# Retention in half chunks on 64x64 quarters of the TensorE array, beside a Strassen feed-forward network

## The chip, the cores and the metric

The kernel runs on 1 core of one Trainium2 chip. The metric is the device time in microseconds (us) of one execution, as a median over the runs of a kernel. A profile is one execution, so a profile's span and the median differ by a few us.

PE is TensorE, the engine for matrix products, and the *array* is what it multiplies in. DVE and ACT (VectorE and ScalarE) do sums, masks and copies, POOL is GpSimd. Transfers (DMA) bring data from memory (HBM) to the buffer beside the engines, whose 128 rows are called partitions; a *bank* is a part of the memory that PE writes its products to. In the profile each 32-bit product leaves two records and each transpose one; counts such as x32 are records.

## The reference, cut to what matters

Retention (attention with a decay in place of the softmax) for 8 batches, 8 heads, 576 positions, head size 64. Its output, as 4608 tokens of 512 features, goes through a feed-forward network with a squared ReLU:

```python
scores = scale * np.matmul(q, k.transpose(0, 1, 3, 2))      # (8, 8, 576, 576)
Dmat = np.where(rel >= 0, gamma[:, None, None] ** rel[None, :, :], 0.0)
x = np.matmul(scores * Dmat, v)                             # -> (4608, 512)
h = np.maximum(x @ w_in, 0.0)                               # w_in  (512, 2048)
out = h * h @ w_out                                         # w_out (2048, 512)
```

The kernel computes the network's matrix products by Strassen's scheme, seven products of blocks and some sums in place of eight products. All arrays that count here are 32-bit floats, except that the weights arrive as 64-bit floats and are converted on the chip.

## The kernel before

The retention runs by chunks of 128 positions, five a batch (the last has 64), 40 in all. For a chunk, x is the sum of two things: what lies within the chunk (masked scores times v) and what comes from all earlier chunks through a state u, which grows by k times v with each chunk. One *visit* of the outer loop does one piece of each of three neighbouring chunks, with pieces of the feed-forward network (`ffn`, made of steps h) and of the weight conversion (`convert`) between them:

```python
for i in range(N_CH + 2):
    if i >= 2:
        retain(i - 2)          # x of a chunk, then the growth of the state
        convert(2 if i < 6 else 1)
        ffn(i - 2)
    if 1 <= i <= N_CH:
        scores(i - 1)
        convert(1 if i > 1 else 0)
        ffn(i - 2)
    if i + 2 < N_CH:
        load(i + 2)            # q, k, v from HBM
    if i < 4:
        for j in range(...):   # (cut) the first weight pieces
            fetch_w(j)
    if i < N_CH:
        turn(i)                # transposes of q, then of k
        convert(1 if i > 1 else 0)
        ffn(i - 2)
```

The retention's products use half of the array: `scores` takes 64 rows by 128 columns (a head's 64 features are summed), x and the growth take 128 rows by 64 columns.

```python
def scores(i):
    # (cut)
    sc = [pool.tile([128, HP, C], F32, tag=tag, name=f"sc{e}") for e in range(2)]
    for hp in range(HP):
        for e in range(2):
            sl = slice(D * e, D * e + D)
            nc.tensor.matmul(sc[e][:cs, hp, :cs], lhsT=kT[sl, hp, :cs], rhs=qT[sl, hp, :cs], start=True, stop=True)
    # (cut) two masked copies by DVE into ret[0], ret[1]; GpSimd makes vs = v * decay

def retain(i):
    # (cut)
    for hp in range(HP):
        if ci > 0:
            for e in range(2):
                half = slice(D * e, D * e + D)
                nc.tensor.matmul(p[half, hp, :cs], lhsT=u_sb[ci % 2][:, hp, half], rhs=s["qT"][:, hp, :cs], ...)
        for e in range(2):
            half = slice(D * e, D * e + D)
            nc.tensor.matmul(p[half, hp, :cs], lhsT=s["vs"][:cs, 2 * hp + e, :], rhs=s["ret"][e][:cs, hp, :cs], ...)
    # (cut) ACT copies p to xT; then the 8 products of the growth, and ACT copies the state
```

The first weight matrix comes in 16 pieces of 512 KB, one transfer each:

```python
return moe_w_in.rearrange("(c p) f -> p c f", p=128)[:, :, f:f + 128]      # piece_src(j)
nc.sync.dma_start(raw_of(j).bitcast(I64)..., piece_src(j))                  # fetch_w(j)
```

Of the kernel before, what the change touches and what calls it, by code (L numbers as in the profile page):

```python
# [9 lines left out]
F32 = mybir.dt.float32  # L10
U32 = mybir.dt.uint32
I64 = mybir.dt.int64
AF = mybir.ActivationFunctionType
ALU = mybir.AluOpType

C = 128
TOK = 512
HT = TOK // 2

# [20 lines left out]
def kernel(  # L40
# [29 lines left out]



    nc = tc.nc
    ctx.enter_context(tc.manual_schedule())

    B, H, S, D = q.shape
    HP = H // 2
# [3 lines left out]
    N_DM = d_model // 128  # L81
# [6 lines left out]
    NCH = -(-S // C)  # L88
    chunks = [(b, ci, ci * C, min(C, S - ci * C)) for b in range(B) for ci in range(NCH)]
    N_CH = len(chunks)  # L90
# [8 lines left out]
    ld4 = first.enter_context(tc.tile_pool(name="ld4", bufs=4))  # L99
    work = first.enter_context(tc.tile_pool(name="work", bufs=1))  # L100
    work2 = first.enter_context(tc.tile_pool(name="work2", bufs=2))
    ps_a = first.enter_context(tc.tile_pool(name="ps_a", bufs=3, space=PS))
    ps_u = first.enter_context(tc.tile_pool(name="ps_u", bufs=1, space=PS))


# [18 lines left out]
    def load(i):  # L124
        b, ci, c0, cs = chunks[i]
        loaded[i] = []
        for name, src, pool in (("q", q, ld3), ("k", k, ld4), ("v", v, ld3)):
            t = pool.tile([128, H, D], F32, tag=name, name=f"{name}_ld")
            nc.sync.dma_start(t[:cs], src[b, :, c0:c0 + cs, :].rearrange("h s d -> s h d"))  # L129
            loaded[i].append(t)  # L130
            if i == 0 and name == "q":
                nc.sync.dma_start(dq[:, :, 0:C], decay_q[:, :, 0:C])
            if i == 0 and name == "k":
                nc.sync.dma_start(dv, decay_v)
        if i == 0:
            nc.sync.dma_start(dq[:, :, C:], decay_q[:, :, C:])
# [15 lines left out]
    def raw_of(j):  # L152
        return raw_all[j % N_RAW] if j < N_W1 else raw_all[(j - N_W1) % 3]
# [4 lines left out]
    def piece_src(j):  # L158
        wi, m, e = pieces[j]
        f = (m + e * N_M) * 128  # L160
        if wi == 0:
            return moe_w_in.rearrange("(c p) f -> p c f", p=128)[:, :, f:f + 128]
        return moe_w_out[f:f + 128, :].rearrange("p (c f) -> p c f", c=N_DM)

    def piece_dst(j):
# [6 lines left out]
    def as_dst(j, t):  # L172

        if pieces[j][0] == 0:
            return t.rearrange("p (c f) -> p c f", c=N_DM)
        return t.rearrange("p (o s f) -> p o s f", o=2, s=2)

    def fetch_w(j):
        if j < len(pieces) and wide:
            nc.sync.dma_start(raw_of(j).bitcast(I64).rearrange("p (c f) -> p c f", c=N_DM), piece_src(j))  # L180



# [1 line left out]
    def round_parts(j):  # L185
# [24 lines left out]
            nc.vector.scalar_tensor_tensor(bits, as_dst(j, hi), 0x80000000, bits, op0=ALU.bitwise_and, op1=ALU.bitwise_or)  # L210

        if not wide:
            return [lambda: nc.sync.dma_start(t, as_dst(j, piece_src(j).rearrange("p c f -> p (c f)")))] + [None] * 4
        return [one, two, three, four, five]

    def sum_w_in(mp):
# [65 lines left out]
    def convert(count):  # L282
        for _ in range(count):
            f = next(w_in_steps, None)
            f and f()
# [8 lines left out]
    ident = only.tile([128, 128], F32, name="ident")  # L294
    make_identity(nc, ident)

    msk = only.tile([128, 1, C], F32, name="msk")
    nc.gpsimd.memset(msk, 1.0)
    nc.gpsimd.affine_select(
        out=msk[:, 0, :], in_=msk[:, 0, :], compare_op=ALU.is_ge, fill=0.0, base=0,  # L300
        pattern=[[1, C]], channel_multiplier=-1,
    )

    u_sb = [only.tile([128, HP, 128], F32, name=f"u_sb{j}") for j in range(2)]
    for t in u_sb:
        nc.gpsimd.memset(t, 0.0)



# [3 lines left out]
    xT = {n: xT_room[n % 2 if n < 2 else (n - 3) % 2] for n in range(N_BLK)}  # L313
    xT[2] = W[6][:, 0:N_DM * TOK].rearrange("p (c t) -> p c t", c=N_DM)

    def turn(i):

        cs, c0 = chunks[i][3], chunks[i][2]
        for j, name in enumerate(("qT", "kT")):
            p = ps_a.tile([128, HP, C], F32, tag="a", name=f"{name}_ps")  # L320
            for hp in range(HP):
                nc.tensor.transpose(p[:, hp, :cs], loaded[i][j][:cs, 2 * hp:2 * hp + 2, :], ident[:cs, :cs])  # L322
            t = st[i][name] = (work if j else work2).tile([128, HP, C], F32, tag=name, name=name)
            if j == 0:
                nc.vector.tensor_tensor(t[:, :, :cs], p[:, :, :cs], dq[:, :, c0:c0 + cs], op=ALU.mult)
            else:
                nc.scalar.copy(t[:, :, :cs], p[:, :, :cs])

    def scores(i):

        b, ci, c0, cs = chunks[i]
        qT, kT = st[i]["qT"], st[i]["kT"]
        pool, tag = (ps_f, "f") if i < TOK // C else (ps_a, "a")
        sc = [pool.tile([128, HP, C], F32, tag=tag, name=f"sc{e}") for e in range(2)]
        for hp in range(HP):
            for e in range(2):
                sl = slice(D * e, D * e + D)
                nc.tensor.matmul(sc[e][:cs, hp, :cs], lhsT=kT[sl, hp, :cs], rhs=qT[sl, hp, :cs],  # L338
                                 start=True, stop=True)
        st[i]["ret"] = []  # L340
        for e in range(2):
            r = work.tile([128, HP, C], F32, tag=f"ret{e}", name=f"ret{e}")
            nc.vector.tensor_tensor(r[:cs, :, :cs], sc[e][:cs, :, :cs],  # L343
                                    msk[:cs, :, :cs].to_broadcast([cs, HP, cs]), op=ALU.mult)
            st[i]["ret"].append(r)
        vs = st[i]["vs"] = work.tile([128, H, D], F32, tag="vs", name="vs")
        nc.gpsimd.tensor_tensor(vs[:cs], loaded[i][2][:cs],  # L347
                                dv[:cs, :, ci:ci + 1].to_broadcast([cs, H, D]), op=ALU.mult)

    def retain(i):  # L350

        b, ci, c0, cs = chunks[i]
        s = st[i]
        p = ps_a.tile([128, HP, C], F32, tag="a", name="x_ps")


        for hp in range(HP):
            if ci > 0:
                for e in range(2):
                    half = slice(D * e, D * e + D)  # L360
                    nc.tensor.matmul(p[half, hp, :cs], lhsT=u_sb[ci % 2][:, hp, half], rhs=s["qT"][:, hp, :cs],  # L361
                                     start=(hp == 0), stop=False, skip_group_check=True)
            for e in range(2):
                half = slice(D * e, D * e + D)
                nc.tensor.matmul(p[half, hp, :cs], lhsT=s["vs"][:cs, 2 * hp + e, :],  # L365
                                 rhs=s["ret"][e][:cs, hp, :cs], start=(ci == 0 and hp == 0), stop=True,
                                 skip_group_check=True)
        tok = b * S + c0
        at = tok
        while at < tok + cs:  # L370
            n = at // TOK
            end = min(tok + cs, (n + 1) * TOK)
            nc.scalar.copy(xT[n][:, :, at - n * TOK:end - n * TOK], p[:, :, at - tok:end - tok])
            at = end
        if ci + 1 < NCH:
            if ci == 0:
                u_ps[0] = ps_u.tile([128, HP, D], F32, tag="u", name="u_ps")
            for hp in range(HP):
                for e in range(2):
                    nc.tensor.matmul(u_ps[0][D * e:D * e + D, hp, :], lhsT=loaded[i][1][:cs, 2 * hp + e, :],  # L380
                                     rhs=s["vs"][:cs, 2 * hp + e, :], start=(ci == 0 and hp == 0),
                                     stop=(hp == HP - 1), skip_group_check=True)
            u = u_sb[(ci + 1) % 2]
            for e in range(2):
                half = slice(D * e, D * e + D)
                nc.scalar.copy(u[half, :, half], u_ps[0][half, :, :])
        st[i] = loaded[i] = None


# [137 lines left out]
    def step():  # L527
        n, f, *args = steps.pop(0)
        f(*args)
# [17 lines left out]
    n_late = [5]  # L547

    for i in range(N_CH + 2):
        if i >= 2:  # L550
            b, ci, c0, cs = chunks[i - 2]

            n = (b * S + c0 + cs - 1) // TOK
            while steps and steps[0][0] <= (n - 2 if n > 4 else n - 3):
                step()
            retain(i - 2)
            convert(2 if i < 6 else 1)
            ffn(i - 2)
            while n_next[0] < N_BLK and (n_next[0] + 1) * TOK <= b * S + c0 + cs:
                steps += block_steps(n_next[0])  # L560
                n_next[0] += 1
        if 1 <= i <= N_CH:
            scores(i - 1)
            convert(1 if i > 1 else 0)
            ffn(i - 2)
        if i + 2 < N_CH:
            load(i + 2)
        if i < 4:
            for j in range((0, 2, 4, 5, 6)[i], (0, 2, 4, 5, 6)[i + 1]):
                fetch_w(j)  # L570
        if i < N_CH:
            turn(i)
            convert(1 if i > 1 else 0)
            ffn(i - 2)
    assert n_next[0] == N_BLK
    first.close()

# [177 lines left out]
```

## Time and profile before

The median is 1063.26 us (1062.85 to 1064.64, 3 runs). The kernel has three stages, and I mark them by the start of three kinds of product: the first `h_ps` (the network has its first block of x), the first `h_a` (its main stage, beside the retention) and the first `o_a` (the second matrix; by then the retention is over). These are lines of the timeline of PE before (start, length, engine, line, operation, output<-inputs, tile and shapes, how many):

```profile
44.47 1.88 PE L442 MATMUL h_ps<-room,w 128*128 128x512 f32 x4
...
143.18 1.99 PE L470 MATMUL h_a<-room,w 128*128 128x256 f32 x8
...
660.67 0.50 PE L642 MATMUL o_a<-w,a 128*128 128x128 f32 x3
```

| stage | from, us | length, us | what is in it |
|---|---|---|---|
| start-up | 0 | 44.5 | loads, first conversions, first chunks of the retention |
| block 0 | 44.5 | 98.7 | `h_ps` steps, retention, conversion of the rest of `w_in` |
| main | 143.2 | 517.5 | `h_a`, `h_b`, `h_c` steps and the other retention |
| last | 660.7 | 402.4 | `o_*` steps, no retention |

### The profile page before, as it was taken

To read this page: it belongs to the slowest core of one execution; us is meant where nothing else is said; L and a number is where in the kernel's file an instruction comes from. 1 tells how busy PE (TensorE), PEld (TensorE's weight loads), DVE (VectorE), ACT (ScalarE), POOL (GpSimd) and SP (SyncE) were. 2 spreads that over 40 slices of the span, in tenths; PEclk is the share of its full clock that TensorE was granted. 3 is DMA by queue.
4 is the path that set the end of the run, shared out by engine and by line. 5 is a ranking of instruction groups with operands and counts; after the bars stand their busy time and mean duration, and the time that the engine had idled before them with its cause. 6 is when DMAs were issued, how large, how long until landed. Compare 5 with 4: busy or idle time off the path is not lost.

```text
span 1063.1 us, 19280 instructions
## 1 busy us (share of the span) xinstructions
PE 1024.7 (96%) x8072; PEld 908.5 (85%) x8072; DVE 775.6 (73%) x1454; ACT 186.1 (18%) x435; POOL 82.0 (8%) x83
## 2 busy tenths in 40 slices
PE   6898979999999999989999999899999999999998
PEld 5665558888888888878878888899999999999998
DVE  3678767766888888886897577677676776776775
ACT  3443312111212222212221100001000000000000
POOL 2101001111011111111011100000000000000000
PEclk9898989999999999999999999999999999999999
DMA  9958654644578868668656798945636546365451
GB/s 242 236 133 208 140 202 139 183 142 150 145 209 256 221 174 286 204 168 262 177 158 216 259 379 312 374 164 195 232 127 236 187 171 238 139 226 202 149 199 40
DMA packets 176070, 214.78 MB, mean 202 GB/s; under 512 B 115312, under 2 KB 124528, under 8 KB 167024
## 3 DMA queue, kind: packets, MB, share of 16 engines
q1 hardware_dynamic: 175984, 213.56, 63.4%
q8 instruction: 63, 1.03, 0.4%
q14 instruction: 23, 0.19, 0.1%
HBM read 125.19 MB, written 88.34 MB: 201 GB/s over the span
## 4 chain that ended last, share of the span: by engine, by line
PE 88%; DVE 6%; DMA 3%; SPq 1%; issue 1%; ACT 1%; DVEq 0%
PE h_b L470 16%; PE o_b L642 15%; PE h_c L470 11%; PE o_c L642 10%; PE o_a L642 10%; PE h_a L470 10%; PE h_ps L442 4%; PE x_ps L365 3%; PE sc L338 3%; PE x_ps L361 3%; PE kT_ps L322 1%; DMA a<-g_dram 1%; DMA k_ld<-in_k_dram 1%; PE qT_ps L322 1%; PE u_ps L380 1%; SPq L129 1%
## 5 line engine op out<-in xcount | busy, mean ns | idle before, releaser
L470 PE MATMUL h_b<-room,w 128*128 128x256 f32 x736 | 177.8, 385 | 14.1 <-DVE room L406 14.1
L470 PEld LDWEIGHTS h_b<-room,w 128*128 128x128 f32 x736 | 138.9, 192 | 35.5 <-issue 12.1
L642 PE MATMUL o_b<-w,room 128*128 128x128 f32 x1168 | 144.5, 275 | 0.2 <-DVE room L614 0.2
L642 PEld LDWEIGHTS o_b<-w,room 128*128 128x128 f32 x1168 | 137.2, 192 | 0.5 <-DVE room L614 0.4
L642 PE MATMUL o_c<-w,room 128*128 128x128 f32 x1008 | 123.0, 275 | 0.0
L642 PEld LDWEIGHTS o_c<-w,room 128*128 128x128 f32 x1008 | 117.7, 192 | 0.0
L470 PE MATMUL h_c<-room,w 128*128 128x256 f32 x480 | 115.8, 385 | 0.0
L470 PE MATMUL h_a<-room,w 128*128 128x256 f32 x448 | 108.0, 384 | 0.0
L470 PEld LDWEIGHTS h_c<-room,w 128*128 128x128 f32 x480 | 90.1, 192 | 12.6
L470 PEld LDWEIGHTS h_a<-room,w 128*128 128x128 f32 x448 | 83.2, 190 | 12.0
L642 PE MATMUL o_a<-w,a 128*128 128x128 f32 x688 | 85.9, 275 | 2.6 <-DMA a<-g_dram 2.6
L642 PEld LDWEIGHTS o_a<-w,a 128*128 128x128 f32 x688 | 81.3, 192 | 2.8 <-issue 2.8
L477 DVE SCALAR_TENSOR_TENSOR room<-room 128x512 f32<-128x512 f32 x96 | 68.1, 710 | 3.3
L489 DVE TENSOR_TENSOR room<-h_b,room 128x512 f32<-128x512 f32 x32 | 22.1, 691 | 57.3 <-PE h_b L470 57.3
L487 POOL TENSOR_TENSOR room<-room 128x512 f32<-128x512 f32 x32 | 34.5, 1078 | 374.1 <-ACT room L486 374.1
L653 ACT COPY r<-o_a 128x128 f32<-128x128 f32 x54 | 14.4, 266 | 276.6 <-PE o_a L642 230.2
L365 PE MATMUL x_ps<-ret,vs 128*64 128x128 f32 (+1 forms) x640 | 60.0, 278 | 1.3 <-DVE ret L343 1.2
L347 POOL TENSOR_TENSOR vs<-v_ld,dv 128x512 f32<-128x512 f32 (+1 forms) x40 | 45.7, 1143 | 200.6 <-issue 86.4
L442 PE MATMUL h_ps<-room,w 128*128 128x512 f32 x128 | 59.7, 610 | 0.0
L343 DVE TENSOR_TENSOR ret<-sc,msk 128x512 f32<-128x512 f32 (+1 forms) x80 | 47.0, 628 | 14.7 <-PE sc L338 14.7
L361 PE MATMUL x_ps<-qT,u_sb 128*64 128x128 f32 (+1 forms) x512 | 50.5, 274 | 0.0
L338 PEld LDWEIGHTS sc<-qT,kT 64*128 64x128 f32 (+1 forms) x640 | 37.0, 183 | 14.9 <-issue 12.6
(92 smaller groups left out, 1374.2 us busy)
## 6 DMA issues: line engine op xcount, KB each, us to landing
g_dram<-room SPq DMA_DIRECT2D x36, 1792.0 KB, 7.3
a<-g_dram SPq DMA_DIRECT2D x43, 1024.0 KB, 6.5
room<-g_dram SPq DMA_DIRECT2D x20, 1024.0 KB, 5.7
w<-w_dram SPq DMA_DIRECT2D x7, 1792.0 KB, 10.8
out_dram<-room SPq DMA_DIRECT2D x18, 512.0 KB, 3.2
q_ld<-in_q_dram SPq DMA_DIRECT2D x32, 256.0 KB, 6.1
k_ld<-in_k_dram SPq DMA_DIRECT2D x32, 256.0 KB, 6.6
v_ld<-in_v_dram SPq DMA_DIRECT2D x32, 256.0 KB, 6.1
```

The source lines that it names most:

```text
L322: nc.tensor.transpose(p[:, hp, :cs], loaded[i][j][:cs, 2 * hp:2 * hp + 2, :], ident[:cs, :cs])
L338: nc.tensor.matmul(sc[e][:cs, hp, :cs], lhsT=kT[sl, hp, :cs], rhs=qT[sl, hp, :cs], start=True, stop=True)
L343: nc.vector.tensor_tensor(r[:cs, :, :cs], sc[e][:cs, :, :cs], msk[:cs, :, :cs].to_broadcast([cs, HP, cs]), op=ALU.mult)
L347: nc.gpsimd.tensor_tensor(vs[:cs], loaded[i][2][:cs], dv[:cs, :, ci:ci + 1].to_broadcast([cs, H, D]), op=ALU.mult)
L361: nc.tensor.matmul(p[half, hp, :cs], lhsT=u_sb[ci % 2][:, hp, half], rhs=s["qT"][:, hp, :cs], start=(hp == 0), stop=False, skip_group_chec ...
L365: nc.tensor.matmul(p[half, hp, :cs], lhsT=s["vs"][:cs, 2 * hp + e, :], rhs=s["ret"][e][:cs, hp, :cs], start=(ci == 0 and hp == 0), stop=Tr ...
L442: nc.tensor.matmul(p.rearrange("p h t -> p (h t)"), lhsT=w[:, c, :], rhs=xT[0][:, c, :], start=(c == 0), stop=(c == N_DM - 1))
L470: nc.tensor.matmul(p[:, mm, :], lhsT=w[:, c, :], rhs=xs[n][right][:, c, :], start=(j in OPENS and mm == 0 and c == 0), stop=(j in CLOSES a ...
L477: nc.vector.scalar_tensor_tensor(t, t, 0.0, t, op0=ALU.max, op1=ALU.mult)
L487: nc.gpsimd.tensor_tensor(g["A11"], g["A11"], g["A11"], op=ALU.mult)
L489: nc.vector.tensor_tensor(g["A22"], p, p15, op=ALU.add)
L642: nc.tensor.matmul(p, lhsT=s["lefts"][left][:, m, :], rhs=w_out[j][:, m, WO_SLOT[right], :], start=(i in OPENS and m == 0), stop=(i in CLO ...
```

## The change

The intent: cut each chunk into halves of 64 positions, so that every retention product fits a 64x64 quarter of the array, and order the products so that neighbours fall on four different quarters and run together. The products of a visit are now three groups: (a) within and growth of the second half, (b) state and scores, (c) within and growth of the first half. Scores and x share one pair of banks, the mask is one DVE copy a chunk, and the transposes have one bank. Q and k are turned between the groups. And because the features of x come out in another order, the rows of `w_in` are permuted, which takes two transfers of 64 partitions for each weight piece.

```diff
+    HEADS = [(g, e, b, 4 * b + 2 * g + e) for g in range(H // 4) for e in range(2) for b in range(2)]
 def scores(i):
+        for hp in range(HP):
+            for h in range(n_h):
+                for e in range(2):
+                    t = slice(CH * h, CH * h + CH)
+                    nc.tensor.matmul(sc[rows(h), e, hp, :], lhsT=kT[rows(e), hp, t], rhs=qT[rows(e), hp, t], ...)
+    # groups a and c: pairs of "own" (within) and "grow" products in turn
+        for j in range(0, len(own), 2):
+            for f in own[j:j + 2] + grow[j:j + 2]:
+                f()
 # (cut: retain_b, retain_c, masks, buffers)
 def piece_src(j):
-            return moe_w_in.rearrange("(c p) f -> p c f", p=128)[:, :, f:f + 128]
+            return moe_w_in.rearrange("(b c d) f -> b d c f", b=2, c=N_DM)[:, :, :, f:f + 128]
+    def bring(t, j):
+        for b in range(2 if pieces[j][0] == 0 else 1):
+            if pieces[j][0] == 0:
+                nc.sync.dma_start(t[64 * b:64 * b + 64], src[b])
 for i in range(N_CH + 2):
+        visit(i)                      # takes the pair of banks
+        if i >= 2:
+            retain_a(i - 2)
+        if i < N_CH:
+            turn(i, "kT")
+        convert(1 if i > 1 else 0); ffn(i - 2)          # (two lines made one)
+        if i >= 2:
+            retain_b(i - 2)
+        if 1 <= i <= N_CH:
+            scores(i - 1)
+        if i < N_CH:
+            turn(i, "qT")
+        convert(1 if i > 1 else 0); ffn(i - 2)
         if i >= 2:
-            retain(i - 2)
+            retain_c(i - 2)
             convert(2 if i < 6 else 1)
             ffn(i - 2)
-        if 1 <= i <= N_CH:
-            scores(i - 1) ...
         if i + 2 < N_CH:
             load(i + 2)
         ...                           # fetch_w as before
-        if i < N_CH:
-            turn(i) ...
```

## The prediction

> **What bounds the kernel now.** I read the page first: busy shares, the 40 slices, the chain that ended last. Then the stretches, to see where TensorE (PE) is not full, and the timeline of PE in a settled stretch, to price one visit of the retention.
>
> ```profile
> PE 1024.7 (96%) x8072; PEld 908.5 (85%) x8072; DVE 775.6 (73%) x1454; ACT 186.1 (18%) x435; POOL 82.0 (8%) x83
> ...
> PE   6898979999999999989999999899999999999998
> ...
> PE 88%; DVE 6%; DMA 3%; SPq 1%; issue 1%; ACT 1%; DVEq 0%
> ```
>
> PE is busy 96% of 1063 us and is 88% of the chain. From about 150 us on its slices are full, so there PE time saved is time saved. Before that it is less simple: in the stretches to 60 us the DMA share is 0.99 to 1.17, and from 60 to 140 us DVE is busy 14.4 to 16.5 us of each 20 (it converts the weights). After 614 us there is no retention at all, so the last 450 us cannot change. What can change are the x_ps, sc and u_ps products, spread over the first 600 us.
>
> Busy sums mislead for them, because records overlap. I price by start times instead. An FFN step h is 8 records and starts 1.725 us before the next one. From the timeline at 203 and 221 us (start, length, engine, line, operation):
>
> ```profile
> 203.46 1.89 PE L470 MATMUL h_b<-room,w 128*128 128x256 f32 x8
> 205.28 1.16 PE L338 MATMUL sc<-qT,kT 64*128 64x128 f32 x16
> 206.38 1.99 PE L470 MATMUL h_c<-room,w 128*128 128x256 f32 x8
> 208.21 1.03 PE L470 MATMUL h_b<-room,w 128*128 128x256 f32 x4
> ```
>
> ```profile
> 221.17 1.89 PE L470 MATMUL h_b<-room,w 128*128 128x256 f32 x8
> 222.99 0.44 PE L361 MATMUL x_ps<-qT,u_sb 128*64 128x128 f32 x4
> 223.26 0.39 PE L365 MATMUL x_ps<-ret,vs 128*64 128x128 f32 x4
> ...
> 224.78 0.64 PE L380 MATMUL u_ps<-vs,k_ld 128*64 128x64 f32 x16
> 225.35 1.99 PE L470 MATMUL h_a<-w,w 128*128 128x256 f32 x8
> 227.18 1.03 PE L470 MATMUL h_b<-room,w 128*128 128x256 f32 x4
> ```
>
> Scores: from h_b to h_b is 4.75 us, less two steps (3.45) leaves **1.30 us**. x and u: 6.01 - 3.45 = **2.56 us**. Inside, 16 records of u_ps take 0.57 us up to the next h; their start times in the trace come in pairs about 7 ns apart, one pair each 58 ns. The 128-column records come in pairs each 109 ns. So two products run next to each other, and a pair costs the time of one. What the pairs don't explain is a fixed cost of a group: 1.30 - 8 x 0.111 = 0.41 for scores; 2.56 - 16 x 0.109 - 8 x 0.058 = 0.35 for x and u; 0.35 for the 64-row scores. I take **0.36 us a group**.
>
> **What the Trainium skill says.** "TensorEngine Tiling (Array Packing)", Tiling Modes, Key Properties: 64x64 gives four independent tiles that load and multiply in parallel, and "Changing tiling mode (not just tile) drains the TensorE". The trace shows two at a time and the fixed cost; four it does not show. "TensorE: Matmul & The Clock Gate", Part 3: packed matmuls start some 4 ns apart but keep strict order. Here they start 7 ns apart, and the order is not strict between tiles: at 21 us a product held up by its operand pairs with the next product of the other half, so each half seems to have its own queue. The same page, Part 1 ("Wait — 56ns, not 53.3ns?"), says start-to-start never falls below about 25 ns on average; the u_ps rate of 29 ns lies just above that, so this trace cannot tell. This is my largest doubt. The tiling page's Gotcha 1 says that different row tiles must not write one PSUM bank together; the change gives each row half its own bank, so that should cost nothing.
>
> **The change part by part**, for 24 full chunks with a state from before, 8 first chunks of a batch, 8 last chunks of 64 rows.
> Before, without the transposes (these stay): full 1.30 + 2.56 = 3.86 us. First chunk, no state product: 1.30 + 1.69 = 2.99 (h_b at 193.14 to h_b at 198.28 is 5.14). Half chunk: scores 0.82; x 2.31 (h_b at 287.30 to h_c at 293.06, less 3.45), because it changes between 128-row and 64-row mode eight times. In all 24 x 3.86 + 8 x 2.99 + 8 x 3.13 = 141.6 us.
> After: the program order shows 5220 products in place of 4196, 1024 more, so more records of half the columns, in three groups a visit: within plus state growth of the second half, state plus scores, within plus growth of the first half. If four run together, 8 records in a quadrant cost 8 x 0.0583 = 0.47 us. Full chunk: 8 + 16 + 8 = 32 rounds = 1.87 plus three groups 1.08 = 2.95. First chunk: 28 rounds, 2.71. Half chunk: 8 (scores, only two quadrants) + 4 + 8 = 20 rounds and two groups, 1.89. In all 70.8 + 21.7 + 15.1 = 107.6 us. **PE saves 34.0 us**: 0.91 a full chunk, 0.28 a first one, 1.24 a half one.
> On the path: the first 13 chunks lie in the stretch that DMA and DVE also pace. The order shows there the last group of one visit directly followed by the first group of the next, with no FFN step between. Both use the single pair of banks, so the second must wait for ACT's copy to xT (0.58 us busy, about 1 us with the hand-over). I count a quarter of their 10.6 us, 2.6. The other 27 chunks: 16 x 0.91 + 5 x 0.28 + 6 x 1.24 = 23.4 us. Sum 26.
> Beside it: DVE makes one masked copy of 128x512 a chunk where it made two (80 at 628 ns become 40), about 23 us less on an engine at 73%. This shortens DVE's queue and a little of the 14.1 us that PE waits for DVE's sums of x: +2. Against it: one bank for the transposes, DVE's read of the scores in the banks that the last group writes, three later places where groups touch: -3. Sixteen more, smaller weight fetches: nothing. Net 25 us: **1038 us**.
>
> **Rivals.**
> (1) The four quadrants don't run together, or the instruction supply caps them. With pairs only, a full chunk has 128 records at 29.2 ns, 3.74 + 1.08 = 4.82, which is 0.96 worse. With 25 ns it has 3.20 + 1.08 = 4.28, 0.42 worse. Half chunks gain still. That makes 1070 to 1090 for the first and about 1068 to 1075 for the second. For it: 25 ns is stated, and four at a time is not in the trace. Against it: the 7 ns stagger, two independent queues already, and groups small enough to lie in the queue before they start. I give all of this 15%, and a middle (18 to 20 ns a record, 1045 to 1055) another 15%.
> (2) New waits eat the gain: a visit is now a ring through ACT (state copy), DVE (mask), ACT (xT), in one pair of banks. For it: DVE is 85% busy from 300 to 400 us, and the single banks. Against it: two FFN steps, 3.4 us, stand between most groups, and a copy takes 0.6. It would leave 1045 to 1055.
> (3) All of the 34 us arrive, with DVE's relief on top, because the early stretch is bound by PE after all (PE is busy 20.0 of 20 us in several of its stretches): about 1026.
>
> **Range and chances.** 1038 us, 8 in 10 between 1022 and 1062: the low end is rival 3 with a bit more, the high end the mild forms of rivals 1 and 2. The border of 2% is at 1042, close to the middle; so faster 0.57, within 2% 0.39, slower 0.04 (only if quadrants don't overlap).
>
> **What would show it.** Right: PE records 10120 (2 x 4900 + 320 transposes); a group of 32 small products between FFN steps costs about 0.83 us, state plus scores 1.29; starts in fours, 58 ns apart; DVE about 750 us; the time after the last retention unchanged at about 450 us, and the gain between 150 and 600 us about 23. Wrong: groups at 1.3 us (pairs) or at 25 ns a record; PE waiting for ACT's xT or u_sb copies or for DVE's ret by more than 5 us after 150 us; a start-up that is longer by more than 5 us.

## More of the kernel before

The *granted clock* is the share of its full clock that PE ran at.

PE waits in the first two stages mostly for loads. The view of PE's waits before, 0 to 143 us (who waits for what: us in total, times, longest):

```profile
PE qT_ps L322 <- DMA q_ld<-in_q_dram: 6.1, 3, 3.9
PE kT_ps L322 <- DVE ret L343: 4.0, 1, 4.0
PE kT_ps L322 <- DMA k_ld<-in_k_dram: 2.9, 4, 2.0
```

## The result, and the profile after

The changed kernel takes **1056.24 us** (median of 4 runs, 1055.54 to 1058.56) against 1063.05 of the kernel before in the same rounds. The ratio is **0.9936**, 95% interval 0.9917 to 0.9956. A ratio here and below is the mean time of one kernel's fast runs over the mean of the other's in the same rounds, so not quite the ratio of the medians. It is a gain of 0.6%, within the 2% band; 25 us were predicted.

Busy shares and PE's slices after (engine, busy us, share, records; then tenths in 40 slices of the span):

```profile
PE 996.0 (95%) x10120; PEld 876.6 (83%) x10120; DVE 748.5 (71%) x1414; ACT 184.7 (18%) x436; POOL 78.5 (7%) x82
...
PE   4699796999999999999999999899999999999998
```

The records of PE (10120) and the busy time of DVE (748.5) are as predicted. But PE's row begins with 4 and 6 where before it began with 6 and 8. The stage marks in the timeline of PE after:

```profile
55.43 1.13 PE L511 MATMUL h_ps<-room,w 128*128 128x512 f32 x2
...
155.95 1.89 PE L539 MATMUL h_a<-room,w 128*128 128x256 f32 x8
...
651.33 0.94 PE L722 MATMUL o_a<-w,a 128*128 128x128 f32 x7
```

| stage | before, us | after, us | difference | predicted |
|---|---|---|---|---|
| start-up | 44.5 | 55.4 | +11.0 | the two together: -2.6 |
| block 0 | 98.7 | 100.5 | +1.8 | |
| main | 517.5 | 495.4 | -22.1 | -22.4 |
| last | 402.4 | 402.5 | 0.0 | 0 |
| profiled span | 1063.1 | 1053.8 | -9.3 | -25 |

So the main stage did what was computed, and **the first two stages lost 12.8 us where they were to gain 2.6**. Two views of the start-up show how. First, engine by engine over the first minute of the span (stretch, its length, then busy us and records of PE, PEld, DVE, ACT and POOL, then the granted clock of PE as a share, the DMA share and GB/s); before:

```profile
0.00:30.00 30.00, 19.91 (x224) 16.71 (x224) 11.48 (x21) 10.90 (x20) 6.39 (x15) 1.00 1.08 234
30.00:60.00 30.00, 27.50 (x262) 19.49 (x263) 20.33 (x38) 12.77 (x27) 4.53 (x4) 0.89 1.04 236
```

and after:

```profile
0.00:30.00 30.00, 15.28 (x280) 12.34 (x284) 6.23 (x12) 7.71 (x13) 5.53 (x14) 0.86 1.06 217
30.00:60.00 30.00, 21.45 (x403) 16.35 (x400) 14.86 (x26) 9.68 (x21) 4.46 (x4) 0.63 0.94 180
```

In both kernels the transfer engines are full in the first 30 us (a share of about 1), and no other engine is: this stretch is bound by transfers. After the change the share is 1.06 and then 0.94, little less, but the bytes are fewer by more: 217 for 234 GB/s, then 180 for 236. From 30 to 60 us PE was nearly full before (27.5 of 30) and is idle for almost a third of the time after; its clock is lower too. Second, PE's waits after, 0 to 156 us:

```profile
PE kT_ps L342 <- DMA k_ld<-in_k_dram: 19.0, 6, 7.0
PE x_ps L392 <- DVE ret L378: 6.5, 3, 4.6
PE x_ps L392 <- ACT room L451: 5.0, 6, 1.2
PE x_ps L392 <- ACT w L451: 4.3, 4, 2.2
```

The transposes of k wait 19.0 us for their loads, where those of q and k together waited 6.1 + 2.9 = 9.0 us before. (ACT at L451 is the copy of x out of the shared banks.)

The mechanism itself can be read from one visit in the settled stretch after, as in the prediction:

```profile
225.27 1.89 PE L539 MATMUL h_b<-room,w 128*128 128x256 f32 x8
227.09 0.27 PE L392 MATMUL x_ps<-ret,v_ld 64*64 64x64 f32 x2
227.10 0.27 PE L398 MATMUL u_ps<-v_ld,k_ld 64*64 64x64 f32 x2
227.19 0.23 PE L392 MATMUL x_ps<-ret,v_ld 64*64 64x64 f32 x2
...
227.71 1.99 PE L539 MATMUL h_c<-room,w 128*128 128x256 f32 x8
229.54 1.89 PE L539 MATMUL h_a<-w,w 128*128 128x256 f32 x8
```

From h_b to h_a there are two steps and one group: 4.27 - 3.45 = **0.82 us** for 32 records, which are 16 products (predicted 0.83). The two x_ps and two u_ps records start within 20 ns of each other, the next four about 0.1 us later, and from there on they come four each 58 ns. The group of state and scores, from 242.84 to 246.25 us with one step and 0.44 us of transposes, took about 1.25 us (predicted 1.29).

### The profile page after: what moved, and what is told of

Same layout as the page of the kernel before. It is cut to its first block, busy times and chain, and to the rows that moved or that the text cites. A ratio compares the mean times of both kernels' runs of the same rounds, so it can differ in the third digit from the quotient of the medians.

```text
span 1053.8 us, 23361 instructions
## 1 busy us (share of the span) xinstructions
PE 996.0 (95%) x10120; PEld 876.6 (83%) x10120; DVE 748.5 (71%) x1414; ACT 184.7 (18%) x436; POOL 78.5 (7%) x82
## 3 DMA queue, kind: packets, MB, share of 16 engines
q8 instruction: 79, 1.29, 0.5%
## 4 chain that ended last, share of the span: by engine, by line
PE 87%; DVE 5%; DMA 5%; ACT 1%; SPq 1%; issue 1%; DVEq 0%; ACTq 0%
PE h_b L539 16%; PE o_b L722 15%; PE h_c L539 10%; PE o_c L722 10%; PE o_a L722 10%; PE h_a L539 10%; PE h_ps L511 5%; DMA k_ld<-in_k_dram 3%; PE x_ps L392 3%; PE kT_ps L342 2%; PE x_ps L430 2%; PE qT_ps L342 2%; PE x_ps L375 1%; DMA a<-g_dram 1%; PE u_ps L398 1%
## 5 line engine op out<-in xcount | busy, mean ns | idle before, releaser
L392 PEld LDWEIGHTS x_ps<-ret,v_ld 64*64 64x64 f32 x1152 | 44.5, 146 | 44.0 <-issue 33.3
L392 PE MATMUL x_ps<-ret,v_ld 64*64 64x64 f32 x1152 | 54.6, 238 | 20.0 <-ACT room L451 8.3
L558 DVE TENSOR_TENSOR room<-h_b,room 128x512 f32<-128x512 f32 x32 | 22.1, 691 | 46.5 <-PE h_b L539 46.5
L380 POOL TENSOR_TENSOR v_ld<-v_ld,dv 128x512 f32<-128x512 f32 (+1 forms) x40 | 43.5, 1090 | 97.7 <-DMA v_ld<-in_v_dram 87.0
L378 DVE TENSOR_TENSOR ret<-x_ps,msk 128x512 f32<-128x512 f32 (+1 forms) x40 | 27.4, 685 | 32.0 <-PE x_ps L375 26.5
L398 PE MATMUL u_ps<-v_ld,k_ld 64*64 64x64 f32 x1024 | 47.5, 237 | 0.0
```

Source lines behind the costliest of these rows:

```text
L378: nc.vector.tensor_tensor(r[:cs], sc[:cs], msk[:cs].to_broadcast([cs, 2, HP, CH]), op=ALU.mult)
L380: nc.gpsimd.tensor_tensor(vs[:cs], vs[:cs], dv[:cs, :, ci:ci + 1].to_broadcast([cs, H, D]), op=ALU.mult)
L392: own.append(lambda g=g, e=e, b=b, head=head: nc.tensor.matmul(x_at(g, e, b, h), lhsT=s["vs"][rows(h), head, :], rhs=s["ret"][rows(h), e, ...
L398: grow.append(lambda hp=hp, e=e, head=head: nc.tensor.matmul(u_ps[0][rows(e), hp, :], lhsT=loaded[i][1][rows(1 - h), head, :], rhs=s["vs"] ...
L558: nc.vector.tensor_tensor(g["A22"], p, p15, op=ALU.add)
```

## The experiments

Two theories for the 12.8 us, and a third for what is left. **A**: k is needed early, so its place in the queue or the late release of its buffer stalls PE (the growth in group c, at the end of a visit, still reads k). **B**: the two 64-partition transfers of a weight piece are slower than one of 128, and this stage is bound by transfers. **C**: PE meets ACT's and DVE's copies more often, because all groups share one pair of banks. Medians are given with the ratio to the kernel before in the same call (1063.05, 1064.37, 1065.11 and 1065.12 us in the four calls); "first h_ps" and "first h_a" are the stage marks of that run's profile, where the change has 55.4 and 156.0.

### 1. Five buffers for k, and k first in the queue

```diff
-        for name, src, pool in (("q", q, ld3), ("k", k, ld4), ("v", v, ld4)):
+        three = (("q", q, ld2), ("k", k, ld5), ("v", v, ld4))   # shortened: q has 2 buffers, k 5
+        for name, src, pool in three if i < 2 else (three[1], three[0], three[2]):
```

> The changed kernel with five buffers for k in place of four (q has two in place of three to make room; k is loaded first). Theory A, late release: the changed kernel turns k at the start of a visit but gives k's buffer back only at the visit's end, so in the start-up each k load waits for a product and each visit waits for the load. Then the 19 us of waits for k in the first 60 us fall to under 10, the first FFN product starts at about 45 to 48 us (55.4 in the changed kernel) and the time is about 1045 to 1049. Theory B, the weight fetches cut into halves of 64 partitions hold up the loads: no change, 1054 to 1058. Theory C, the ring of groups through ACT and DVE in one pair of banks sets the start-up: no change beyond 3 us.

Measured: 1054.28 us, ratio 0.9914 (0.9897 to 0.993); first h_ps 54.6, first h_a 154.6; PE waits 21.1 us for k, no less than the 19.0 of the change. The release of a buffer is not what k waits for. This half of A falls.

### 2. Turn k after the scores and q at the end of the visit

```diff
-            turn(i, "kT")       # after group a
...
-            turn(i, "qT")       # after the scores
+            turn(i, "kT")
...
+        if i < N_CH:            # after group c, before the loads and the fetches
+            turn(i, "qT")
```

> The changed kernel with both turns a third of a visit later (k after the scores, q after the last group); buffers as they are. Theory A: each load has a third of a visit more, waits for k in the start-up fall by half or more, 1046 to 1051. Theory B: 1054 to 1058. Theory C: about 1056, or slower, since nothing stands any more between the first group and the state product that needs ACT's copy.

Measured: 1054.11 us, 0.9915 (0.99 to 0.993); first h_ps 53.0, first h_a 151.6, so 4.3 us of the 12.8 are back. The waits for k were to halve and fall to 15.4. Less than half of the 4.3 us is left at the end: the main stage became 1.6 us longer (496.9 for 495.4) and the last 1.9 (404.4 for 402.5), the latter for a reason that run 12 shows. So the place of the turns does count, though less than A had it.

### 3. A whole fetch of each weight piece (wrong result)

The rows of `w_in` are not permuted, so the output is wrong; the bytes are the same.

```diff
-            return moe_w_in.rearrange("(b c d) f -> b d c f", b=2, c=N_DM)[:, :, :, f:f + 128]
+            return moe_w_in.rearrange("(c p) f -> p c f", p=128)[:, :, f:f + 128]
...
-                nc.sync.dma_start(t[64 * b:64 * b + 64], src[b])
+        nc.sync.dma_start(t, src)
```

> The changed kernel with each piece of w_in fetched by one DMA over 128 partitions as before the change (rows not permuted, so the result is wrong on purpose). Theory A: 1054 to 1058, first FFN product at 54 to 56 us. Theory B: about 1045, first FFN product before 50 us. Theory C: 1054 to 1058.

Measured: 1053.21 us, 0.991 (0.9895 to 0.9925); first h_ps 50.5, first h_a 153.5. The start-up gets 5.0 us shorter, but both numbers that B had expected were missed (first h_ps before 50, about 1045 us), and PE still waits 18.4 us for k. The issues of the weights after, and with whole pieces, in the view of the transfers (KB each, median us from issue to landing):

```profile
w<-in_moe_w_in_dram SPq DMA_DIRECT2D x32, 256.0 KB, 5.2
```

```profile
w<-in_moe_w_in_dram SPq DMA_DIRECT2D x16, 512.0 KB, 5.1
```

Half a piece takes as long to land as a whole one; by itself this shows little, since that time also holds the wait behind earlier transfers. The packets say more: by the trace's records between 10 and 50 us, a packet of 1 KB takes 56 ns on average in the kernel before and 59 here, but 76 in the change. That speaks for B.

### 4. The kernel before, with three buffers for k

```diff
-    ld4 = first.enter_context(tc.tile_pool(name="ld4", bufs=4))
+    ld4 = first.enter_context(tc.tile_pool(name="ld4", bufs=3))
```

> The kernel before with three buffers for k in place of four, so that a k load waits for the retention of the chunk one later. Theory A: the start-up of the kernel before gets longer in the same way, first FFN product at 50 us or later (44.5 before), 1068 to 1076. Theories B and C: within 3 us of 1063.

Measured: 1069.04 us, 1.0054 (1.0039 to 1.0069). Some 6 us slower, but not where A looks for it: first h_ps at 42.4 us is 2 us earlier than before, and the main stage takes 524.1 us. By its time alone the run would have passed for support; by its stages it is none. Of the 6.6 us that the main stage lost, 3.0 are longer waits for DVE (17.1 us for 14.1), and PE's clock was at 0.50 for two stretches of 3.41 us there (from 417 and 478 us), which the kernel before has nowhere after 157 us in that stage: at most 1.7 us each. Why DVE is later stays open.

### 5. The kernel before, with half fetches

Only the transfers of the change, in the kernel before; the result is right.

```diff
-            nc.sync.dma_start(raw_of(j)..., piece_src(j))
+            for at in (slice(0, 64), slice(64, 128)) if pieces[j][0] == 0 else (slice(0, 128),):
+                nc.sync.dma_start(t[at], piece_src(j)[at])
```

> The kernel before with each piece of w_in fetched by two DMAs over 64 partitions, as the changed kernel does, rows not permuted; nothing else. Theory B (the halves move the same bytes more slowly: packets of 1 KB took 72 to 84 ns in the changed kernel's start-up and 52 to 61 ns before): packets of 70 to 85 ns here too, first FFN product 3 to 6 us later than 44.5, time 1064 to 1069. If instead the order of the visit alone sets the start-up: first FFN product within 1 us of 44.5 and 1062 to 1064.

Measured: 1070.72 us, **1.0059** (1.0044 to 1.0074), so 6.4 us slower, a little more than B expected; first h_ps 50.0 for 44.5, first h_a 149.8 for 143.2, and nothing after that (main stage 517.7 for 517.5). Packets of 1 KB take 76 ns on average, as in the change. PE's waits in this run, 0 to 150 us:

```profile
PE qT_ps L324 <- DMA q_ld<-in_q_dram: 9.1, 3, 4.1
PE kT_ps L324 <- DVE ret L345: 4.0, 1, 4.0
PE x_ps L367 <- DVE ret L345: 3.5, 1, 3.5
```

**This confirms B**: one part of the change, alone, costs 6.4 us in this kernel, the slow packets come with it, and PE waits 9.1 us for q, which stands in the same queue, where it waited 6.1. Whether it is the 64 partitions or the doubled number of transfers, no run separates: runs 10 and 11 were to, and failed for another reason. The Trainium skill has this in two places. "SBUF — State Buffer", section Door 1, says that partitions 0 to 63 reach only the 8 even of 16 ports, and 64 to 127 the 8 odd ones. "DMA: Bandwidth & Descriptors", Rules for kernel authors, says of two transfers to disjoint partition halves: "Don't bother — they serialize", and to use one of 128. The trace agrees so far as a half moves its bytes more slowly (packets of 76 ns for 56, so 1.4 times and not twice). The ports themselves no run here shows.

### 6. Weight fetches after the loads of a visit

In the change a visit takes its conversion steps, which queue further weight pieces, before it queues the loads of chunk i+2: eight pieces stand ahead of the seventh chunk's loads, before it was seven.

```diff
-                    fetch_w(j + N_RAW)
+                    later.append(j + N_RAW)
...
+        while later:                 # at the end of the visit, after load(i + 2)
+            fetch_w(later.pop(0))
```

> The changed kernel with the weight fetches that the conversion asks for issued after the visit's q, k and v loads instead of among the steps before them. Theory D (in the changed kernel one more 512 KB piece stands ahead of the seventh chunk's loads in the one DMA queue): waits for k fall by some 2 to 4 us, first FFN product at 51 to 54 us (55.4), time 1052 to 1055. If the order in the queue does not matter: 55 us and 1056.

Measured: 1055.21 us, 0.9912 (0.9895 to 0.993); first h_ps 53.1, first h_a 153.5. PE still waits 19.0 us for k. It brings 2.4 us by the main stage and no more: the order in the queue is a small term.

### 7. Neighbouring products on only two quarters

To see what the quarters themselves are worth: the same products, ordered so that neighbours fall on two quarters.

```diff
-        for j in range(0, len(own), 2):
-            for f in own[j:j + 2] + grow[j:j + 2]:
-                f()
+        for f in own + grow:
+            f()
# likewise e outermost in the scores and in the state products
```

> The changed kernel with the same products put in an order in which neighbours use only two quadrants (all of within, then all of the growth; state and scores first for one row half, then for the other). If four run together only when they are neighbours: groups of 32 cost 1.3 us in place of 0.8 and state plus scores 2.2 in place of 1.3, in all 30 to 50 us more, 1086 to 1106. If each quadrant has its own queue and PE looks far enough ahead, the order hardly matters: 1056 to 1065.

Measured: 1077.88 us, 1.0128 (1.0095 to 1.0162). The main stage takes 511.4 us for 495.4. A group, in the timeline of PE of this run:

```profile
230.49 1.89 PE L537 MATMUL h_b<-room,w 128*128 128x256 f32 x8
232.31 0.51 PE L392 MATMUL x_ps<-ret,v_ld 64*64 64x64 f32 x10
232.60 0.27 PE L398 MATMUL u_ps<-v_ld,k_ld 64*64 64x64 f32 x2
232.65 0.28 PE L392 MATMUL x_ps<-ret,v_ld 64*64 64x64 f32 x3
...
232.77 0.51 PE L398 MATMUL u_ps<-v_ld,k_ld 64*64 64x64 f32 x11
...
235.04 1.89 PE L537 MATMUL h_a<-w,w 128*128 128x256 f32 x8
```

4.55 - 3.45 = 1.10 us, between 0.82 (fours) and 1.29 (pairs all along). Growth records (u_ps) start at 232.60 us, and six of the sixteen records of the products within (x_ps), all of which stand before them in the program, start only after that, from 232.65 us on. So here some products went ahead of others, but not all that could have: the time lies between the two expectations, and the order of the program is worth about 16 us in the main stage. The four quarters do run together.

### 8. The kernel before, with fewer changes of mode in its half chunks

The prediction put a cost on changes of tile shape. Before, x of a 64-row chunk changes it eight times; this edit makes it twice.

```diff
+        if cs < C:
+            for f in (past, own):      # all state products, then all within
+                for hp in range(HP):
+                    f(hp)
```

> The kernel before with the last chunk of a batch (64 rows) ordered so that all state products come before all products within, two changes of tile mode in place of eight. If the mode changes cost what the trace suggests (some 0.15 us each), this x stage falls from 2.31 to about 1.45 us, 0.86 x 8 = 7 us of PE, of which 5 to 7 on the path: 1056 to 1058, as much as the whole change gave. If the cost is something else: within 2 us of 1063.

Measured: 1062.08 us, 0.9977 (0.9961 to 0.9992). One such x, in the timeline of PE of this run:

```profile
285.56 1.89 PE L481 MATMUL h_b<-room,w 128*128 128x256 f32 x8
287.38 0.69 PE L360 MATMUL x_ps<-qT,u_sb 128*64 128x64 f32 x16
288.00 0.68 PE L366 MATMUL x_ps<-ret,vs 64*64 64x64 f32 x16
288.61 1.99 PE L481 MATMUL h_c<-room,w 128*128 128x256 f32 x8
290.44 1.89 PE L481 MATMUL h_a<-room,w 128*128 128x256 f32 x8
```

4.88 - 3.45 = 1.43 us where it took 2.31: six changes less, about 0.15 us each. The main stage is 5.6 us shorter, which is what six half chunks at 0.88 us give (5.3). At the end 4.3 us of it are left in the profiled run (1058.8 for 1063.1), since the last stage has 1.8 us more, and by the medians 2.3. The expected time was missed; the last stage, explained in run 12, is one reason, and the spread of the runs (1060.53 to 1063.52) leaves the rest open.

### 9. Turns at the end of the visit, for the first 13 chunks only

```diff
-            turn(i, "kT")                  # after group a
+            if i >= 13:
+                turn(i, "kT")
...
-            turn(i, "qT")                  # after the scores
+            if i >= 6:
+                turn(i, "qT" if i >= 13 else "kT")
...
+        if i < 13:                         # at the end of the visit
+            if i < 6:
+                turn(i, "kT")
+            turn(i, "qT")
```

> The changed kernel with the turns of the first six chunks at the end of the visit, as before the change, those of the next seven a third of a visit later, the others where the change has them. Theory E: PE takes its instructions in order, and the change put k's turn at the head of a visit, so a late k also holds up the products of older chunks that stand behind it. Then the first FFN product starts at 47 to 52 us (55.4), the waits for ACT's xT copy before 160 us fall by half, and the time is 1047 to 1052. If only the amount and speed of the transfers matter: 53 to 56 us and 1053 to 1056.

Measured: 1054.28 us, 0.99 (0.9882 to 0.9919); first h_ps 53.4, first h_a 152.6. Of k's turns only the first six stand at the end, the next seven after the scores. The waits for k go down from 19.0 to 12.9 and those for ACT's copies of x from 9.3 to 3.4, but those for DVE's masked scores go up from 6.5 to 10.6. 3.3 us of the 12.8 are back. The start-up (47 to 52) and the time (1047 to 1052) that theory E expected were both missed; both numbers are those of its rival, that only the transfers count. So PE's waits moved more than they shrank. (That PE takes its instructions in order is true only roughly: see run 7.)

### 10. and 11. Permuted weights by four 128-partition transfers

An attempt at a right result with whole transfers: a piece as four transfers, one for each group of columns. Alone (10), and with the turns and the fetch order mended (11).

```diff
-            for b in range(2): ...
-                nc.sync.dma_start(t[64 * b:64 * b + 64], src[b])
+            for c in range(N_DM):
+                nc.sync.dma_start(t[:, c, :], src[:, :, c, :])
```

> The changed kernel with each piece of w_in fetched by four DMAs over all 128 partitions (one for each column block) in place of two over 64; the rows come out permuted as the change needs, so the result is right. Theory B (it is the 64 partitions that make the packets slow): 1 KB packets take 52 to 62 ns, as in the run with whole fetches: 1051 to 1054. If it is the number of DMAs: packets as slow as with halves or slower, 1056 to 1060.

> The changed kernel with all three mends: later turns at the start, weight fetches issued after the loads, fetches over 128 partitions. If the three causes are separate and add up: first FFN product at 42 to 47 us, first step of the second stage at about 142 us, and with the 495 us and 403 us that the other stages take in the changed kernel about 1040 to 1046, faster than both kernels. If they overlap: 1047 to 1052.

Measured: 1171.14 us (1.1005) and 1164.34 us (1.0941). A stretch of the first of them, columns as above:

```profile
20.00:30.00 10.00, 0.86 (x24) 0.55 (x16) 0.22 (x1) 0.00 (x0) 0.00 (x0) 0.66 0.13 47
```

47 GB/s at a DMA share of 0.13: of 16 engines about two work. The source's leading dimension has size 2 (the two row halves), and "DMA: Bandwidth & Descriptors", Rules for kernel authors, says that the slowest dimension that is not 1 sets the number of engines. 0.13 x 16 = 2.1 agrees. So these runs say nothing of partitions against number of transfers, and run 11 nothing of its other two edits. No run here has a right result with whole transfers.

### 12. All three mends, with the whole fetch (wrong result)

Edits 3, 6 and 9 together.

> The changed kernel with later turns at the start, weight fetches issued after the loads, and whole fetches over 128 partitions with unpermuted rows (result wrong on purpose): all three suspected causes of the longer start-up taken away. If they add up (alone they brought the first FFN product forward by 2.0, 2.3 and 4.9 us): first FFN product at 45 to 48 us, second stage from 143 to 148 us, time 1042 to 1048. If something else also holds the start-up: first FFN product at 49 us or later and over 1049.

Measured: 1049.58 us, **0.9857** (0.9833 to 0.9881); first h_ps 48.4, first h_a 146.2. The second mark is as expected (143 to 148), the first (45 to 48) and the time (1042 to 1048) are not. Of the 12.8 us, 9.8 are gone. PE's waits for k are down to 9.2 (those for DVE's masked scores are up from 6.5 to 10.1), and the transfers are faster: between 20 and 40 us they move 241 GB/s, where the change moves 201 and the kernel before 253. But the last stage is 3.2 us longer (405.7 for 402.5). In every kernel here PE waits once in that stage, some 17 us after its start, between 2.4 and 2.95 us for one transfer. What differs is what follows. The 4 us after that wait, in the change and then in this run (columns as above):

```profile
671.33:675.33 4.00, 4.00 (x39) 4.00 (x38) 3.96 (x11) 0.27 (x1) 0.00 (x0) 1.00 1.02 430
```

```profile
662.14:666.14 4.00, 4.00 (x20) 4.00 (x21) 3.75 (x9) 0.27 (x1) 0.00 (x0) 0.50 1.01 426
```

At a granted clock of 0.50 PE leaves 20 records in place of 39, and in the next 4 us 29 of 39: together 29 records are missing, at 4 us for 39 that is 3.0 us, nearly all of the 3.2. In runs 2 and 8 it is 23 and 24 of 39 in one such stretch, about 1.6 us of their 1.9 and 1.8.

The length of the wait doesn't decide it: 2.9 us in these three runs, but also in runs 1 and 4, which have no drop, and 2.4 in run 13, which has one. Its place does; no run was made for this, but the kept traces show it. In each of the 16 traces the changes of the granted clock lie whole multiples of 3.41 us apart, so I cut the time into windows of 3.41 us at these points. The two windows that hold the wait, in run 1 and then in this run (columns as above):

```profile
664.91:668.33 3.42, 1.89 (x17) 1.69 (x16) 0.00 (x0) 0.27 (x1) 0.00 (x0) 1.00 0.98 411
668.33:671.74 3.41, 2.01 (x18) 2.04 (x19) 2.09 (x6) 0.27 (x1) 0.00 (x0) 1.00 1.02 432
```

```profile
657.82:661.24 3.42, 1.18 (x11) 0.98 (x9) 0.00 (x0) 0.27 (x1) 0.00 (x0) 1.00 1.00 421
661.24:664.65 3.41, 2.72 (x13) 2.75 (x14) 2.80 (x7) 0.27 (x1) 0.00 (x0) 0.50 1.01 428
```

Both waits are 2.93 us long. In run 1 the window edge cuts its wait into 1.53 and 1.40 us, in run 12 into 2.24 and 0.69. Over all traces: in the seven with a drop (runs 2 and 8 to 13) 2.04 to 2.86 us of the wait lie in one window, and the clock is at 0.50 from its end on; in the nine without, never more than 1.79. No edit here aims at that place, so the 3.2 us are luck, and so is it that neither of the two main kernels lost them.

### 13. The two mends that keep the result right

Edits 6 and 9 together; the fetch stays in halves.

> The same without the last of the three: halves of 64 partitions and permuted rows, as the change has them, so the result is right. First FFN product at 50 to 53 us, time 1049 to 1053. The difference to the run with all three is what the cut fetches cost the changed kernel: 4 to 6 us if it carries through as in the kernel before (6.4 us).

Measured: **1051.79 us, 0.9881** (0.9848 to 0.9914), right result; first h_ps 51.1, first h_a 150.1. It beats the kernel before by 1.2%, still within the 2% band. Its interval against the kernel before does not meet that of the change (0.9917 to 0.9956), which was run in another call, not side by side. Against 12 it tells the fetch apart: 150.1 - 146.2 = 3.9 us by the main stage (4 to 6 were expected), 2.2 by the medians (in the profiles run 12's last stage is 2.0 us longer, by the clock). Run 12 also had the lower clock in the start-up (0.50 for 1.00 between 20 and 40 us), so 3.9 may be too little.

### 14. The second halves from another queue

Run 13, with the second half of each piece issued by ACT.

```diff
-                nc.sync.dma_start(t[64 * b:64 * b + 64], src[b])
+                (nc.scalar if b else nc.sync).dma_start(t[64 * b:64 * b + 64], src[b])
```

> As the run before it, with the second half of each fetch issued from ACT's queue, so that both halves of the partitions are in flight together. If the halves are slow because only 64 partitions are written at a time: 1 KB packets take 52 to 65 ns and the time is 1045 to 1050. If each half is slow for itself: packets of 72 to 84 ns and 1049 to 1055, or more if ACT's queue is held up by the wait for DVE.

Measured: 1053.87 us, 0.9905 (0.9871 to 0.9939); first h_ps 55.5, first h_a 155.0. The packets of 1 KB take 79 to 100 ns, longer than ever. Two halves at once do not make a whole: each gets slower, and the start-up is 4.4 us longer than in run 13. The reading that a half is slow only because 64 partitions are written at a time had 52 to 65 ns and falls short; but the transfers also stand in another engine's queue here, so it is not refuted.

## Why the prediction was right or wrong

**What bounds the kernel** (right from 150 us on). The main stage became 22.1 us shorter, the last stage did not change (402.4 and 402.5). The prediction's "about 450 us" for the rest after the last retention contains the last 47 to 50 us of h steps.

**What four quarters cost** (right, and this was the largest doubt). A group in 0.82 us (0.83 predicted; the prediction calls its 32 records products, they are 16 of two records each), state and scores in about 1.25 (1.29), fours each 58 ns. Rival 1 falls by this and by run 7, in which the order alone is worth 16 us in the main stage. Run 8 confirms that the half chunks lost time to mode changes.

**The sum for the main stage** (right, with a little luck). Saved 23.4, DVE's relief 2, new waits -3 were predicted. PE's waits in the stage, first before and then after:

```profile
PE h_b L470 <- DVE room L406: 14.1, 6, 6.2
```

```profile
PE h_b L539 <- DVE room L475: 11.0, 3, 8.7
PE x_ps L392 <- ACT room L451: 3.4, 4, 1.0
PE x_ps L392 <- ACT u_sb L441: 0.4, 1, 0.4
PE x_ps L392 <- DVE ret L378: 0.3, 1, 0.3
```

The relief is 14.1 - 11.0 = 3.1 us, the new waits are 4.1, and the difference to 22.1 leaves 23.1 us for the products, as a remainder and not measured by itself. The two waits were each 1.1 us larger than thought, and cancel. Rival 2 was real and about as small as the prediction had it.

**The first 13 chunks** (wrong; this is the step that failed). The prediction wrote "I count a quarter of their 10.6 us, 2.6", and for the transfers "Sixteen more, smaller weight fetches: nothing". In place of +2.6 - 0 the runs show -12.8. The prediction had itself read the DMA share of 0.99 to 1.17 in the stretches to 60 us, and yet priced the stretch by PE's work. Its last sentence names the sign that came true: a start-up longer by more than 5 us. Rival 3, that this stretch would give all of its 10.6 us, fails by the same stretch. That 1056 us still lies between 1022 and 1062 is luck: the high end was meant for mild forms of rivals 1 and 2, which did not bring it about. The runs divide the 12.8 us so:

- The halved fetches, sized as nothing: 6.6 us by the main stage when put alone into the kernel before (run 5), 3.9 when taken away last (13 to 12), 2.5 when taken away alone (3), each by the marks of one profiled execution. The size depends on what else holds PE at that time; that it is not nothing is shown three times.
- The moved turns and the fetch order: 5.9 us taken away together (156.0 to 150.1, run 13), 3.3 and 2.4 each alone. The prediction looked at which group follows which; it did not ask what the transposes of k, now near the head of a visit, would wait for.
- 3.0 us remain in run 12. The meetings with ACT and DVE in the one pair of banks (theory C) and a lower clock are both in this stretch, and no run tells them apart. The clock alone doesn't order the runs: run 13 had 1.00 and 0.89 from 0 to 30 and from 30 to 60 us, as the kernel before, and was 6.9 us behind it at the main stage; run 12 had 0.83 and 0.72 and was 3.0 behind. This stays open.

Theory A in its form "the buffer of k comes free too late" is wrong (run 1); in the form "k is needed too early in the visit" it holds a part (runs 2 and 9).

**What is left to the 25 us.** Run 12, with the losses mended, is 15 us better than the kernel before. The other 10 are the 2.6 that never came, the 3.0 just named, 3.2 us of clock drop in the last stage, which is luck (run 12), and about 1 in small terms.

## What to carry to other kernels

A new tile shape on TensorE may not come alone: here it permuted rows of a weight, which halved the partitions of each transfer, and moved the first consumer of a load to the head of its loop body. Price each stage by its own bound: in a stretch with the DMA share at 1, count transfers, their partitions and the place of their first use, and let saved TensorE time count as nothing there. And when a change splits into a part that pays and parts that cost, put each cost alone into the *old* kernel (run 5 here), where nothing else moves. Before a difference of 1 to 3 us is read into an edit, compare the granted clock stage by stage: here one wait, placed otherwise, made the last stage up to 3.2 us longer.

## What the Trainium skill lacked or had wrong

- "TensorE: Matmul & The Clock Gate", Part 3, has packed matmuls start in strict program order. Run 7 shows otherwise: growth records start at 232.60 us ahead of six records of products that stand before them, and the group takes 1.10 us, between fours (0.82) and pairs (1.29).
- The same page, Part 1, gives about 25 ns as the least start-to-start time, while its Part 3 has packed starts some 4 ns apart. With four quarters the 25 ns do not hold in a row either: four records each 58 ns are 14.5 ns a record.
- "TensorEngine Tiling (Array Packing)", Key Properties, says that a change of mode drains TensorE, with no figure. Here: about 0.15 us a change (2.31 to 1.43 us for six fewer).
- "DMA: Bandwidth & Descriptors", Rules for kernel authors, advises against two half transfers; the skill's bandwidths of halves ("SBUF — State Buffer") are of one or two such transfers. No page has what halves cost in a full queue. Here: 1 KB packets of 76 ns for 56 on average, and 6.4 us of 1064 for 16 pieces; from two queues 79 to 100 ns.
- "TensorE: Matmul & The Clock Gate", Part 1, has the clock fall to half after an idle window of about 3.4 us, and its rules warn of gaps over about 3 us. The 3.41 us grid is in the traces here, but a window need not be idle throughout: the clock fell when PE stood still for 2.04 to 2.86 us of one (waits of 2.4 to 2.9 us), and not at 1.53 to 1.79 us (waits of 2.4 to 2.95 us). One such drop made the last stage 1.2 to 3.2 us longer.
